# The product of v's summary with the input weight for all eight heads at once, over 64x32 pieces of the array and two PSUM banks

## The chip, the cores and the metric

One core of a Trainium2 chip runs the whole kernel. The metric is the device time of one execution in microseconds, taken from the first to the last instruction with what lies around them. Inputs and output lie in HBM; the two weights of each feed-forward layer come as 64-bit floats and are turned into 32-bit ones on the core.

## The reference, cut to what matters

For each of 8 batches and 8 heads, with 576 positions, head width 64 and 32 memory slots:

```
a   = softmax(phi)                      # 576 x 32
k_m = a.T @ k ;  v_m = a.T @ v          # 32 x 64 each: the summaries of k and v
attn = softmax(q @ k_m.T / 8)           # 576 x 32
x   = attn @ v_m                        # heads side by side: 576 x 512 per batch
h   = x @ w_in   (512 x 2048);  g = h * sigmoid(1.702 h);  y = g @ w_out   (2048 x 512)
out = the same kind of layer again, on y, with its own weights and sigmoid(h)
```

The kernel never forms x. It multiplies v's summary with the rows of w_in that belong to the head: for head i, v_m[i] (32 x 64) times rows 64i to 64i+63 of w_in. The eight results, 32 x 2048 each, stand over each other as a 256 x 2048 matrix W' of the batch, and h = attn (576 x 256) @ W'. This change is about how W' is computed.

## The kernel before, in words

The first layer runs in 256 numbered **slots**: 8 batches, two halves of 288 positions each, 16 blocks of 128 columns of w_in. In slot s, `first1` (line 386) issues 6 matmuls of 288 columns that give h of one block, `gate` lets ScalarE (lines 360, 364), VectorE (361) and GpSimd (366) make g in a high and a low part, and `second1` (line 398) issues the 12 matmuls of y for slot s-2. Everything else that a batch needs is planned into slots by tables of numbers: `at(slot, when, fn)` puts a call into slot `slot`, at one of the places "e" (ahead of the slot's h), "p" (behind the h, so on TensorE between h and y), "l" and "d" (loads, last). The attention of batch b+1 and its W' are worked out while batch b's slots run, so that a batch takes 32 slots. From slot 34 on the order of instructions is the written one on each engine; before that a scheduler moves them.

W' of a batch is 2048 columns wide and is made in pieces of 512: `c` = 0 to 3 is the piece of columns, `g` = 0, 1 the group of four heads. Before, there are eight products per batch, one for each (c, g). `wp_mm` (lines 273 to 277) takes one PSUM bank and issues two fp32 matmuls; each uses all 128 rows of the array and 64 of its columns. Their left side is the summary of two heads; since `kv_norm` (line 201) writes the summary twice, multiplied by a mask, the left side is block-diagonal and half of it is zero. `wp_hi` (ScalarE, line 281) and `wp_lo` (VectorE, line 285) then take the bank out as a high and a low part into `slab`.

The bank comes from `psa()` (line 90), a pool with **two** PSUM banks that are given out in turn and that all small matmuls of a batch share: the transposes of phi's maximum (`phi_max_t`, read by `phi_max_r`, line 149 on VectorE), its spreading (`phi_max_b`, line 157, read by `phi_sub`, line 164 on VectorE), `kv_mm` (line 185), `kv_t` (209), the transposes of q (`q_t`, line 220, read by `q_e` on ScalarE, line 224), `scores` (line 230, read by `soft1` on VectorE, line 242) and `wp_mm`. A bank comes free when its reader is done.

Per batch, counted from slot 32(b-1), where the slots of the batch ahead begin, the tables put the W' products at 20, 23, 27, 29, 31, 34, 38 and 39 (`WS`); transposes of q at 12, 16, 18, 20, 24, 27, 28 and 30; scores at 18, 23, 29 and 31; and, for the batch after the next, `phi_max_t` at 33, `phi_max_r` at 34, `phi_max_b` at 35, `phi_sub` at 36 and 37, `kv_mm` from 40 on. `soft2` (lines 255 to 260, VectorE) stands at 23, 26, 34 and 35. For batches 0 and 1 tables of their own (`W0`, `W1`) give the slots of the W' products.

w_in lies in SBUF as `w1` (128 x 4 x 2048, fp32). `w1_load` fetches a piece of 128 rows and 512 columns by one DMA, `w1_conv0` and `w1_conv1` (ScalarE, VectorE, GpSimd: lines 77, 78, 85, 86, 88) turn it into fp32. The loads stand in SyncE's queue among those of phi, k, v and q.

The few lines that say it:

```python
def psa():
    return ps_a.tile([128, 512], F32, tag="a", name="a")      # ps_a: bufs=2
WS = (20, 23, 27, 29, 31, 34, 38, 39)
SC = ((18, 19, 23), (23, 24, 26), (29, 30, 34), (31, 32, 35))
```

Of the kernel before, what the change touches and what calls it, by code (L numbers as in the profile page):

```python
# [10 lines left out]
I32 = mybir.dt.int32  # L11
# [3 lines left out]
ALU = mybir.AluOpType  # L15
# [6 lines left out]
def attn_moe_moe(ctx: ExitStack, tc: tile.TileContext, q, k, v, phi, w1i, w1o, w2i, w2o, out):  # L22
    nc = tc.nc
    B, H, S, D = q.shape
# [30 lines left out]
        return ap.bitcast(F32)  # L55


    def wload(src, rows, cols, t):

        if src.dtype == I64:  # L60
            nc.sync.dma_start(out=t.rearrange("p f w -> p (f w)"), in_=src[rows, cols].bitcast(I32))
            return t
        t = t.bitcast(F32).rearrange("p f w -> p (f w)")[:, 0:512]
        nc.sync.dma_start(out=t, in_=src[rows, cols])
        return t

    def raw():
        return moe.tile([128, 512, 2], I32, tag="raw", name="raw", bufs=2)
# [123 lines left out]
    def kv_norm(b, g):  # L192
        a = st.pop(("kvps", b, g))
        rs = att.tile([128, 2], F32, tag="rs", name="rs", bufs=2)
        nc.vector.tensor_scalar(out=rs[:, 0:1], in0=a[:, 2 * D:2 * D + 1], scalar1=1e-9, scalar2=None, op0=ALU.add)
        nc.vector.reciprocal(out=rs[:, 1:2], in_=rs[:, 0:1])
        kvb = att.tile([128, 2, 2, D], F32, tag="kvb", name="kvb")
        keep = mask.rearrange("p (s o) -> p s o", o=1).to_broadcast([128, 2, D])
        for i in range(2):
            x = a[:, i * D:(i + 1) * D].rearrange("p (o d) -> p o d", o=1).to_broadcast([128, 2, D])  # L200
            nc.vector.scalar_tensor_tensor(out=kvb[:, i], in0=x, scalar=rs[:, 1:2], in1=keep,
                                           op0=ALU.mult, op1=ALU.mult)
        st["kvb", b, g] = kvb

    def kv_t(b, g):
# [64 lines left out]
        t = attnT[b, hf]  # L270
        (nc.gpsimd if b else nc.vector).tensor_tensor(out=t[:, g, 1], in0=x, in1=rd(t[:, g, 0]), op=ALU.subtract)

    def wp_mm(b, c, g):
        a = st["wp", b, c, g] = psa()
        for i in range(2):
            nc.tensor.matmul(out=a[64 * i:64 * i + 64], lhsT=st["kvT", b, g][:, 1, 64 * i:64 * i + 64],
                             rhs=w1[:, 2 * g + i, c * 512:(c + 1) * 512], start=True, stop=True)

    def wp_hi(b, c, g):
        t = slab[b, c, g] = moe.tile([128, 2, 512], F32R, tag="slab", name="slab", bufs=8)  # L280
# [21 lines left out]

    def w1_load(n, kk, j):
        st["w1", kk, j] = wload(w1i, rows(kk), cols(j), early(n))

    def w1_conv0(kk, j):
        wconv0(st["w1", kk, j], w1[:, kk, cols(j)])
# [7 lines left out]
    def wo1_load(n, f):  # L315
        st["wo1", f] = wload(w1o, rows(f), cols(0), early(n))
# [384 lines left out]
    STGO = (1, 3, 4, 5)  # L701
    POOLF = (1, 3, 5, 7, 12, 14)

    W0 = (-4, -2, 1, 2, 10, 13, 14, 15)
    W1 = (18, 25, 28, 29, 32, 33, 39, 41)
    WS = (20, 23, 27, 29, 31, 34, 38, 39)

    Z1 = 5
    KV = ((8, 9, 10, 11, 12), (12, 13, 14, 15, 16))
# [14 lines left out]
    def plan_attention(b, z):  # L724
        for g in range(2):
            at(z - 2 + g, "e", phi_max, b, g)
        at(z + 1, "p", phi_max_t, b)
        at(z + 2, "e", phi_max_r, b)
        at(z + 3, "p", phi_max_b, b)
        for g in range(2):  # L730
            at(z + 4 + g, "e", phi_sub, b, g)
            at(z + 5 + g, "e", phi_exp, b, g)
            at(z + 6 + g, "e", phi_sum, b, g)
        for g, (k0, k1, n, t, e) in enumerate(KV):
            at(z + k0, "p", kv_mm, b, g, 0)
            at(z + k1, "p", kv_mm, b, g, 3)
            at(z + n, "e", kv_norm, b, g)
            todo.setdefault((z + t, "p"), []).insert(0, (kv_t, (b, g)))
            at(z + e, "e", kv_e, b, g)
        at(z + 10, "d", load_kv, b, 1, 0)  # L740
        at(z + 11, "d", load_kv, b, 1, 3)
        if b + 1 < B:
            at(z + 14, "d", load_kv, b + 1, 0, 0)
            at(z + 15, "d", load_kv, b + 1, 0, 3)
            at(z + 15, "d", load_phi, b + 1)
        for n in range(8):
            at(z + QS[n], "p", q_t, b, n // 4, n % 4)
            at(z + QS[n] + 1, "e", q_e, b, n // 4, n % 4)
            at(z + (QS[n - 2] if n > 1 else 2 + n), "d", load_q, b, n // 4, n % 4)
        for n, (p, s1, s2) in enumerate(SC):  # L750
            at(z + p, "p", scores, b, n // 2, n % 2)
            at(z + s1, "e", soft1, b, n // 2, n % 2)
            at(z + s1, "l", soft_exp, b, n // 2, n % 2)
            at(z + s2, "e", soft2, b, n // 2, n % 2)
            at(z + s2, "l", soft_hi, b, n // 2, n % 2)
            at(z + s2 + 1, "e", soft3, b, n // 2, n % 2)

    def plan_first(z):
# [9 lines left out]
        for g in range(2):  # L768
            at(z + 4 + g, "p", kv_mm, 0, g, 0)
            at(z + 4 + g, "p", kv_mm, 0, g, 3)  # L770
            at(z + 5 + g, "e", kv_norm, 0, g)
            at(z + 6 + g, "p", kv_t, 0, g)
            at(z + 7 + g, "e", kv_e, 0, g)
# [13 lines left out]
            at(s2, "l", soft_hi, 0, n // 2, n % 2)  # L787
            at(s2 + 1, "e", soft3, 0, n // 2, n % 2)

    def plan_wprime(b, n, s):  # L790
        a = (b,) + divmod(n, 2)
        at(s, "p", wp_mm, *a)
        at(s + 1, "e", wp_hi, *a)
        if b:
            at(s + 2, "e", wp_lo, *a)
        else:
            at(s + 1, "l", wp_lo, *a)

    make_identity(nc, ident)
    nc.vector.memset(ones, 1.0)  # L800
# [26 lines left out]
    for b in range(B):  # L827
        if b:
            plan_attention(b, 32 * (b - 1) + (Z1 if b == 1 else 0))
        for n in range(8):  # L830
            plan_wprime(b, n, (W0, W1)[b][n] if b < 2 else 32 * (b - 1) + WS[n])
    for n, p in enumerate(seq):
        o = CONV[n]
        w = len(p) == 2
# [174 lines left out]
```

## Time and profile before

| | us |
|---|---|
| median of 3 runs | 1595.64 (1595.29 to 1596.5) |
| profiled execution | 1593.76 |
| its span, first to last instruction | 1592.0 |
| slots of the first layer, h of slot 0 to the last h | 34.9 to 816 |
| busy TensorE / VectorE / ScalarE / GpSimd in the span | 1514.9 / 1007.5 / 765.0 / 556.0 |

An execution has a stretch of loading and converting up to about 110 us, then the slots of the first layer at TensorE's pace up to about 820 us, then the second layer. In the rows below L386 is h, L398 is y, L276 is the W' product. A row "x4" of L276 is one product: each fp32 matmul shows as two passes. Times are from the start of the span.

### The profile page before, as it was taken

To read this page: it belongs to the slowest core of one execution; us is meant where nothing else is said; L and a number is where in the kernel's file an instruction comes from. 1 tells how busy PE (TensorE), PEld (TensorE's weight loads), DVE (VectorE), ACT (ScalarE), POOL (GpSimd) and SP (SyncE) were. 2 spreads that over 40 slices of the span, in tenths; PEclk is the share of its full clock that TensorE was granted. 3 is DMA by queue.
4 is the path that set the end of the run, shared out by engine and by line. 5 is a ranking of instruction groups with operands and counts; after the bars stand their busy time and mean duration, and the time that the engine had idled before them with its cause. 6 is when DMAs were issued, how large, how long until landed. Compare 5 with 4: busy or idle time off the path is not lost. (4 is left out here: it accounts for less than half of the span.)

```text
span 1592.0 us, 29090 instructions
## 1 busy us (share of the span) xinstructions
PE 1514.9 (95%) x11104; PEld 1405.9 (88%) x11104; DVE 1007.5 (63%) x1560; ACT 765.0 (48%) x1539; POOL 556.0 (35%) x461
## 2 busy tenths in 40 slices
PE   4799999999999999999999999999977999999998
PEld 2578898988989898898999999999977999999998
DVE  6995546365463645634567655665677678677675
ACT  4674444454554544544555554554654434344342
POOL 2764334344443444433322311311126234044040
PEclk9799999999999999999999999999998999999999
DMA  9652252524425253312125424424454514515330
GB/s 281 184 163 60 56 132 86 142 71 116 119 87 155 75 139 93 93 39 88 42 66 167 140 105 152 142 105 151 154 181 137 188 50 151 163 60 176 108 102 31
DMA packets 174156, 189.08 MB, mean 119 GB/s; under 512 B 50112, under 2 KB 161728, under 8 KB 174016
## 3 DMA queue, kind: packets, MB, share of 16 engines
q1 hardware_dynamic: 174016, 187.22, 38.5%
q8 instruction: 87, 1.43, 0.4%
q14 instruction: 53, 0.43, 0.1%
HBM read 122.16 MB, written 65.01 MB: 118 GB/s over the span
## 5 line engine op out<-in xcount | busy, mean ns | idle before, releaser
L398 PE MATMUL y<-gh,wo 128*128 128x288 f32 x2048 | 460.0, 301 | 0.3 <-ACT gh L364 0.3
L642 PE MATMUL p<-wq,op 128*128 128x256 f32 x3024 | 373.5, 285 | 20.9 <-ACT op L629 10.5
L642 PEld LDWEIGHTS p<-wq,op 128*128 128x128 f32 x3024 | 366.1, 191 | 28.3 <-DVE op L438 15.8
L398 PEld LDWEIGHTS y<-gh,wo 128*128 128x128 f32 x2048 | 341.3, 188 | 52.1 <-issue 25.8
L366 POOL TENSOR_TENSOR gl<-g,gh 128x288 fp32r<-128x288 f32 x256 | 225.4, 881 | 424.6 <-ACT gh L364 377.2
L398 PE MATMUL y<-gl,wo 128*128 128x288 f32 x1024 | 301.8, 295 | 2.7 <-POOL gl L366 2.7
L361 DVE SCALAR_TENSOR_TENSOR g<-g,h 128x288 f32<-128x288 f32 x256 | 114.7, 449 | 288.1 <-ACT g L360 286.7
L438 DVE TENSOR_TENSOR op<-r,op 128x768 fp32r<-128x768 f32 x168 | 217.5, 1323 | 102.3 <-ACT op L629 97.1
L386 PE MATMUL h<-attnT,slab 128*128 128x288 f32 x1536 | 249.7, 297 | 13.7 <-ACT attnT L266 5.7
L386 PEld LDWEIGHTS h<-attnT,slab 128*128 128x128 f32 x1536 | 218.5, 189 | 18.8 <-ACT attnT L266 6.8
L533 PE MATMUL xb<-xq,wq 128*128 128x384 f32 x1152 | 219.5, 339 | 11.4 <-ACT e L566 6.3
L629 ACT CAST op<-r 128x768 fp32r<-128x768 f32 x168 | 138.0, 835 | 187.1 <-DVE r L438 86.3
L533 PEld LDWEIGHTS xb<-xq,wq 128*128 128x128 f32 x1152 | 200.4, 188 | 18.9 <-ACT e L583 9.7
L398 PEld LDWEIGHTS y<-gl,wo 128*128 128x128 f32 x1024 | 192.7, 188 | 4.6 <-POOL gl L366 3.6
L360 ACT ACTIVATE g<-h 128x288 f32<-128x288 f32 x256 | 104.2, 407 | 189.6 <-PE h L386 182.7
L364 ACT CAST gh<-g 128x288 fp32r<-128x288 f32 x256 | 110.7, 433 | 167.6 <-DVE g L361 167.5
L533 PE MATMUL y<-xq,wq 128*128 128x384 f32 x864 | 166.4, 337 | 2.5 <-ACT e L594 2.5
L533 PEld LDWEIGHTS y<-xq,wq 128*128 128x128 f32 x864 | 151.8, 188 | 2.8 <-ACT e L594 2.8
L542 ACT ACTIVATE gq<-e 128x384 f32<-128x384 f32 x144 | 75.0, 525 | 131.9 <-DVE e L435 131.9
L435 POOL TENSOR_TENSOR r<-r 128x768 f32<-128x768 f32 x24 | 57.2, 2411 | 212.5 <-DMA r<-gs 212.4
L547 DVE SCALAR_TENSOR_TENSOR gq<-gq,e 128x384 f32<-128x384 f32 x144 | 99.9, 698 | 32.7 <-ACT gq L542 27.5
L438 POOL TENSOR_TENSOR xq<-xr,xq 128x768 fp32r<-128x768 f32 x20 | 38.5, 1924 | 153.9 <-ACT xq L523 153.9
(111 smaller groups left out, 1523.6 us busy)
## 6 DMA issues: line engine op xcount, KB each, us to landing
gs<-gq SPq DMA_DIRECT2D x192, 192.0 KB, 1.9
r<-gs SPq DMA_DIRECT2D x192, 192.0 KB, 3.9
raw<-in_moe_w_out_dram SPq DMA_DIRECT2D x24, 512.0 KB, 4.0
raw<-in_moe_w_in_dram SPq DMA_DIRECT2D x18, 512.0 KB, 4.7
xr<-xs SPq DMA_DIRECT2D x24, 384.0 KB, 5.0
out_dram<-o SPq DMA_DIRECT2D x24, 384.0 KB, 3.2
q<-in_q_dram SPq DMA_DIRECT2D x124, 72.0 KB, 2.5
kv<-in_k_dram SPq DMA_DIRECT2D x30, 288.0 KB, 4.4
```

The source lines that it names most:

```text
L360: nc.scalar.activation(out=t[:, :n], in_=h[:, :n], func=ACTF.Tanh, scale=c)
L361: nc.vector.scalar_tensor_tensor(out=t[:, :n], in0=t[:, :n], scalar=1.0, in1=h[:, :n], op0=ALU.add, op1=ALU.mult)
L364: nc.scalar.copy(out=gh[:, :n], in_=t[:, :n])
L366: nc.gpsimd.tensor_tensor(out=gl[:, :n], in0=t[:, :n], in1=rd(gh[:, :n]), op=ALU.subtract)
L386: nc.tensor.matmul(out=h[:, :HS], lhsT=slab[b, f // 4, g][:, wi, f0:f0 + 128], rhs=x[:, g, xi], start=(g == 0 and n == 0), stop=(g == 1 an ...
L398: nc.tensor.matmul(out=ybank[d][:, :HS], lhsT=w[:, wi, d * 128:(d + 1) * 128], rhs=gg[gi][:, :HS], start=(f == fa and n == 0), stop=(f == ...
L438: eng.tensor_tensor(out=out, in0=a, in1=b, op=ALU.subtract)
L533: nc.tensor.matmul(out=out, lhsT=w[:, s, wi, f0:f0 + 128], rhs=x[:, s, xi], start=(start and s == 0 and k == 0), stop=(s == 1 and k == 2), ...
L542: nc.scalar.activation(out=t, in_=h, func=ACTF.Tanh)
L547: nc.vector.scalar_tensor_tensor(out=t, in0=t, scalar=1.0, in1=h, op0=ALU.add, op1=ALU.mult)
L629: nc.scalar.copy(out=t[:, :, 0], in_=s)
L642: nc.tensor.matmul(out=out[:, d], lhsT=t[:, u, gi, d * 128:(d + 1) * 128], rhs=w[:, u, wi], start=(start and d != 1 and p == 0 and u == 0 ...
```

## The change

`wp_mm` does both groups of heads in one call: two banks at once, and eight fp32 matmuls per piece of 512 columns, one per head. Each uses 64 rows and 32 columns of the array: head 4g+j lies on rows 64g to 64g+63 and writes partitions 32j to 32j+31 of bank g. There are four products per batch in place of eight. For that, `w1` is laid out anew (`w1[64g : 64g+64, j]` holds the rows of head 4g+j), so that a load of w_in is two DMAs of 64 partitions, and the summary of v is written twice without the mask. The tables are new: per batch the four products stand in slots 21, 25, 34 and 37. `wp_lo` follows `wp_hi` in the same slot.

```diff
+    def wload(src, rows, cols, t, at=slice(0, 128)):
+            nc.sync.dma_start(out=t[at].rearrange("p f w -> p (f w)"), in_=src[rows, cols].bitcast(I32))
 ...
-        for i in range(2):
-            x = a[:, i * D:(i + 1) * D].rearrange("p (o d) -> p o d", o=1).to_broadcast([128, 2, D])
-            nc.vector.scalar_tensor_tensor(out=kvb[:, i], in0=x, scalar=rs[:, 1:2], in1=keep,
-                                           op0=ALU.mult, op1=ALU.mult)
+        x, y = (a[:, i * D:(i + 1) * D].rearrange("p (o d) -> p o d", o=1).to_broadcast([128, 2, D]) for i in range(2))
+        nc.vector.scalar_tensor_tensor(out=kvb[:, 0], in0=x, scalar=rs[:, 1:2], in1=keep, op0=ALU.mult, op1=ALU.mult)
+        nc.vector.tensor_scalar(out=kvb[:, 1], in0=y, scalar1=rs[:, 1:2], scalar2=None, op0=ALU.mult)
 ...
-    def wp_mm(b, c, g):
-        a = st["wp", b, c, g] = psa()
-        for i in range(2):
-            nc.tensor.matmul(out=a[64 * i:64 * i + 64], lhsT=st["kvT", b, g][:, 1, 64 * i:64 * i + 64],
-                             rhs=w1[:, 2 * g + i, c * 512:(c + 1) * 512], start=True, stop=True)
+    def wp_mm(b, c):
+        for g in range(2):
+            st["wp", b, c, g] = psa()
+        for j in range(4):
+            for g in range(2):
+                r = slice(64 * g, 64 * g + 64)
+                nc.tensor.matmul(out=st["wp", b, c, g][32 * j:32 * j + 32], lhsT=st["kvT", b, g][r, 1, 32 * j:32 * j + 32],
+                                 rhs=w1[r, j, c * 512:(c + 1) * 512], start=True, stop=True)
 ...
+        t = early(n)
+        for g in range(2):
+            r = slice(256 * g + 64 * kk, 256 * g + 64 * kk + 64)
+            st["w1", kk, j] = wload(w1i, r, cols(j), t, slice(64 * g, 64 * g + 64))
 ...
-    W0 = (-4, -2, 1, 2, 10, 13, 14, 15)
-    W1 = (18, 25, 28, 29, 32, 33, 39, 41)
-    WS = (20, 23, 27, 29, 31, 34, 38, 39)
+    W0 = (-2, 2, 13, 15)
+    W1 = (26, 30, 37, 39)
+    WS = (21, 25, 34, 37)
 ...
+        at(s, "p", wp_mm, b, c)
+        for g in range(2):
+            at(s + 1, "e", wp_hi, b, c, g)
+            at(s + 1, "e" if b else "l", wp_lo, b, c, g)
```

What moves on the engines is shown at three places. The first is TensorE around slot 130, which is slot 34 of the third batch in the steady part (b = 4). Before, with the product's two matmuls (L276) between h (L386) and y (L398), and `phi_max_b` (L157) in the next slot:

```order
L386 MATMUL h<-attnT,slab 128x288 x5
L276 MATMUL a<-w_83,kvT 64x512 [waits DVE_49]
L276 MATMUL a<-w_83,kvT 64x512
L398 MATMUL y_5559<-gh,wo_306 128x288 [waits DVE_49,Activation_49]
...
L386 MATMUL h<-attnT,slab 128x288 x6
L157 MATMUL a<-ident,nm 96x128 [waits DVE_49,PE_49]
```

And now (h is L394, y is L406, the product L280):

```order
L394 MATMUL h<-attnT,slab 128x288 x5
L280 MATMUL a<-w_83,kvT 32x512 [waits PE_49]
L280 MATMUL a<-w_83,kvT 32x512 [waits DVE_49,PE_49]
L280 MATMUL a<-w_83,kvT 32x512 x6
L406 MATMUL y_5648<-gh,wo_312 128x288 [waits Activation_49]
...
L394 MATMUL h<-attnT,slab 128x288 x6
L157 MATMUL a<-ident,nm 96x128 [waits DVE_49]
```

The second matmul of the product now waits for VectorE: the first one writes the bank of g = 0, the second the bank of g = 1, which `phi_max_t` of slot 33 had.

The second place is VectorE in the same slots: `phi_max_r` (L149), the gate (L361 before, L369 now), `soft2` (L255 to L260), `wp_lo` (L285 before, L289 now) and `phi_sub` (L164). Before:

```order
L149 TENSOR_REDUCE nm<-a 128x2
L361 SCALAR_TENSOR_TENSOR g<-g,h 128x288 [waits Activation_49]
L255 TENSOR_REDUCE sm<-nat 128x9
...
L260 STREAM_TRANSPOSE at<-nat 128x288 [waits DVE_49,Pool_49]
L361 SCALAR_TENSOR_TENSOR g<-g,h 128x288 [waits Activation_49]
L285 TENSOR_TENSOR slab<-a,slab 128x512 [waits PE_49]
L164 TENSOR_TENSOR phi<-phi,a 96x768 [waits PE_49]
```

And now:

```order
L149 TENSOR_REDUCE nm<-a 128x2
L369 SCALAR_TENSOR_TENSOR g<-g,h 128x288 [waits Activation_49]
L255 TENSOR_REDUCE sm<-nat 128x9
...
L260 STREAM_TRANSPOSE at<-nat 128x288 [waits DVE_49,Pool_49]
L289 TENSOR_TENSOR slab<-a,slab 128x512 [waits Activation_49] x2
L369 SCALAR_TENSOR_TENSOR g<-g,h 128x288 [waits Activation_49]
L164 TENSOR_TENSOR phi<-phi,a 96x768 [waits PE_49]
```

Both `wp_lo` of the piece now stand one after the other behind `soft2` and ahead of the gate.

The third place is SyncE's queue at the start, with the first loads of w_in (L61). Before:

```order
L109 DMA kv<-in_v_dram 96x4x192
L61 DMA rawe<-in_moe_w_in_dram 128x1024 x2
L119 DMA kve<-in_k_dram 96x2x192
```

And now:

```order
L109 DMA kv<-in_v_dram 96x4x192
L61 DMA rawe<-in_moe_w_in_dram 64x1024 x4
L119 DMA kve<-in_k_dram 96x2x192
```

Each load of w_in is two DMAs of half the rows; there are 16 such loads in all.

## Rows read from the trace of the kernel before

**Rows 1.** The profile page, part 1: busy time (share of the span) and instructions of each engine.

```profile
PE 1514.9 (95%) x11104; PEld 1405.9 (88%) x11104; DVE 1007.5 (63%) x1560; ACT 765.0 (48%) x1539; POOL 556.0 (35%) x461
```

**Rows 2.** Busy time of each engine by stretch (start:end, length, then PE, PEld, DVE, ACT, POOL with instruction counts, granted clock, DMA share, GB/s).

```profile
0.00:50.00 50.00, 22.31 (x151) 13.48 (x151) 37.36 (x67) 24.45 (x45) 17.83 (x19) 0.82 0.86 248
50.00:110.00 60.00, 51.62 (x354) 40.17 (x354) 59.39 (x94) 42.60 (x90) 42.84 (x35) 0.95 0.63 183
...
324.00:420.00 96.00, 96.00 (x762) 85.67 (x761) 51.94 (x105) 46.58 (x110) 39.39 (x43) 1.00 0.39 106
420.00:516.00 96.00, 96.00 (x763) 85.67 (x762) 51.58 (x104) 45.39 (x108) 40.42 (x44) 1.00 0.39 108
```

**Rows 3.** TensorE in order of time in slots 112 to 120, its h, q, scores and W' rows alone (start, duration, line, x count); the start of an h row is the start of a slot.

```profile
402.24 0.95 PE L386 MATMUL h<-attnT,slab 128*128 128x288 f32 x6
403.03 0.41 PE L220 MATMUL a<-ident,q 96*128 96x96 f32 x3
404.88 0.95 PE L386 MATMUL h<-attnT,slab 128*128 128x288 f32 x6
407.25 0.95 PE L386 MATMUL h<-attnT,slab 128*128 128x288 f32 x6
...
410.70 0.96 PE L386 MATMUL h<-attnT,slab 128*128 128x288 f32 x6
413.09 0.99 PE L386 MATMUL h<-attnT,slab 128*128 128x288 f32 x6
413.92 0.41 PE L220 MATMUL a<-ident,q 96*128 96x96 f32 x3
414.26 1.08 PE L276 MATMUL a<-w,kvT 128*64 128x512 f32 x4
...
416.94 0.96 PE L386 MATMUL h<-attnT,slab 128*128 128x288 f32 x6
...
421.73 0.95 PE L386 MATMUL h<-attnT,slab 128*128 128x288 f32 x6
422.61 0.71 PE L230 MATMUL a<-qT,kvT 128*64 128x288 f32 x4
423.15 1.03 PE L276 MATMUL a<-w,kvT 128*64 128x512 f32 x4
425.79 0.43 PE L386 MATMUL h<-attnT,slab 128*128 128x288 f32 x2
```

**Rows 4.** TensorE in order of time at three places: one matmul of a product alone (two passes, early in the program), a whole product (four passes) in slot 130, and `kv_mm`, whose matmuls use 96 rows and four groups of 32 columns.

```profile
85.31 1.07 PE L276 MATMUL a<-w,kvT 128*64 128x512 f32 x2
86.32 1.06 PE L386 MATMUL h<-attnT,slab 128*128 128x288 f32 x6
...
455.46 0.96 PE L386 MATMUL h<-attnT,slab 128*128 128x288 f32 x6
456.35 1.08 PE L276 MATMUL a<-w,kvT 128*64 128x512 f32 x4
457.36 0.40 PE L398 MATMUL y<-gh,wo 128*128 128x288 f32 x1
...
459.04 0.95 PE L386 MATMUL h<-attnT,slab 128*128 128x288 f32 x6
459.82 0.60 PE L157 MATMUL a<-ident,nm 128*96 128x128 f32 x4
...
382.36 0.86 PE L185 MATMUL a<-kv,phi 96*32 96x128 f32 x24
383.15 0.38 PE L189 MATMUL a<-ones,es 96*128 96x2 f32 x2
```

**Rows 5.** VectorE in order of time in slots 130 and 131 (start, duration, line; in brackets what ended idle time before it).

```profile
454.76 0.96 DVE L377 TENSOR_SCALAR o<-y 128x288 f32<-128x288 f32 x2
455.64 0.44 DVE L255 TENSOR_REDUCE sm<-nat 128x9 f32<-128x288 f32 x1
...
457.47 0.32 DVE L149 TENSOR_REDUCE nm<-a 128x2 f32<-128x192 f32 x1
...
460.51 0.48 DVE L260 STREAM_TRANSPOSE at<-nat 128x288 f32<-128x288 f32 x1 [0.69 <-POOL attnT L271]
460.91 0.42 DVE L361 SCALAR_TENSOR_TENSOR g<-g,h 128x288 f32<-128x288 f32 x1
461.25 0.68 DVE L285 TENSOR_TENSOR slab<-a,slab 128x512 fp32r<-128x512 f32 x1
```

**Rows 6.** Slot 133, which is slot 37 of the batch: the start of its h on TensorE, and the second `phi_sub` on VectorE with the weight conversion ahead of it.

```profile
464.22 0.96 PE L386 MATMUL h<-attnT,slab 128*128 128x288 f32 x6
...
465.91 0.69 DVE L86 SCALAR_TENSOR_TENSOR stg<-raw,stg 128x512 int32<-128x512 int32 x1
466.52 0.94 DVE L164 TENSOR_TENSOR phi<-phi,a 96x768 f32<-96x768 f32 x1
```

**Rows 7.** `phi_max_r` on VectorE in slot 98, slot 34 of the batch before, where a weight conversion lies ahead of it; and TensorE's rows of that slot.

```profile
363.66 0.32 DVE L149 TENSOR_REDUCE nm<-a 128x2 f32<-128x192 f32 x1
...
359.79 0.96 PE L386 MATMUL h<-attnT,slab 128*128 128x288 f32 x6
360.67 1.08 PE L276 MATMUL a<-w,kvT 128*64 128x512 f32 x4
```

**Rows 8.** Slot 40, the end of batch 1's W': TensorE's `kv_mm`, and VectorE's end of `soft2` with the `wp_lo` behind it.

```profile
186.28 0.86 PE L185 MATMUL a<-kv,phi 96*32 96x128 f32 x24
...
187.71 0.48 DVE L260 STREAM_TRANSPOSE at<-nat 128x288 f32<-128x288 f32 x1 [0.69 <-POOL attnT L271]
188.11 0.42 DVE L361 SCALAR_TENSOR_TENSOR g<-g,h 128x288 f32<-128x288 f32 x1
188.45 0.68 DVE L285 TENSOR_TENSOR slab<-a,slab 128x512 fp32r<-128x512 f32 x1
```

**Rows 9.** ScalarE behind the transposes of q in slot 116: the copy that frees the bank.

```profile
415.44 0.39 ACT L224 COPY qT<-a 128x288 f32<-128x288 f32 x1
415.73 0.59 ACT L281 CAST slab<-a 128x512 fp32r<-128x512 f32 x1
```

**Rows 10.** SyncE's queue at the start: issues of the first loads (start, time in the queue, x count).

```profile
3.62 1.50 SPq L61 DMA_DIRECT2D rawe<-in_moe_w_in_dram  x2
...
14.38 0.90 SPq L61 DMA_DIRECT2D rawe<-in_moe_w_in_dram  x2
```

More of the change, by code (lines that the diff above doesn't have):

```diff
@@ L55, in rd @@
         return ap.bitcast(F32)
-    def wload(src, rows, cols, t):
+    def wload(src, rows, cols, t, at=slice(0, 128)):
         if src.dtype == I64:
-            nc.sync.dma_start(out=t.rearrange("p f w -> p (f w)"), in_=src[rows, cols].bitcast(I32))
+            nc.sync.dma_start(out=t[at].rearrange("p f w -> p (f w)"), in_=src[rows, cols].bitcast(I32))
             return t
         t = t.bitcast(F32).rearrange("p f w -> p (f w)")[:, 0:512]
-        nc.sync.dma_start(out=t, in_=src[rows, cols])
+        nc.sync.dma_start(out=t[at], in_=src[rows, cols])
         return t
@@ L303, in w1_load @@
     def w1_load(n, kk, j):
-        st["w1", kk, j] = wload(w1i, rows(kk), cols(j), early(n))
+        t = early(n)
+        for g in range(2):
+            r = slice(256 * g + 64 * kk, 256 * g + 64 * kk + 64)
+            st["w1", kk, j] = wload(w1i, r, cols(j), t, slice(64 * g, 64 * g + 64))
     def w1_conv0(kk, j):
@@ L788, in plan_first, with plan_wprime @@
             at(s2 + 1, "e", soft3, 0, n // 2, n % 2)
[L790 to L797, printed above, removed]
+    def plan_wprime(b, c, s):
+        at(s, "p", wp_mm, b, c)
+        for g in range(2):
+            at(s + 1, "e", wp_hi, b, c, g)
+            at(s + 1, "e" if b else "l", wp_lo, b, c, g)
     make_identity(nc, ident)
@@ L829, in attn_moe_moe @@
             plan_attention(b, 32 * (b - 1) + (Z1 if b == 1 else 0))
-        for n in range(8):
+        for n in range(4):
             plan_wprime(b, n, (W0, W1)[b][n] if b < 2 else 32 * (b - 1) + WS[n])
```

## Prediction

> **What bounds the kernel now.** I began with the page's busy times: TensorE is busy 95% of the span, VectorE 63%, ScalarE 48% [rows 1]. An average over stages says little, so next came busy time by stretch [rows 2]. In the steady part, 324 to 516 us, TensorE is busy 96.00 of 96 us twice over and VectorE a little over half. There every microsecond taken off TensorE's queue comes off the time, unless TensorE then waits for something. From 50 to 110 us it is the other way: VectorE is busy 59.39 of 60 us, TensorE 51.62, so less work for TensorE buys nothing there. The third view is TensorE in order of time [rows 3], which gives the price of each kind of slot, and the fourth VectorE's rows at the places where the change makes TensorE wait [rows 5 to 8].
>
> **What is removed.** Differences between starts of h [rows 3]: a plain slot is 407.25 - 404.88 = 2.37 us; with a transpose of q 404.88 - 402.24 = 2.64; with that and scores 410.70 - 407.25 = 3.45, so scores cost 0.81. A slot with a transpose and a product is 416.94 - 413.09 = 3.85, so a product costs 3.85 - 2.64 = 1.21. Behind scores it is cheaper: 425.79 - 421.73 = 4.06, less 2.37 and 0.81, is 0.88. Of a batch's eight products three stand behind scores (slots 23, 29, 31), five don't: 3 x 0.88 + 5 x 1.21 = 8.7 us per batch.
>
> **What is added.** Four products per batch, none in a slot with scores or a transpose. What one costs hangs on whether eight matmuls run side by side in the array. For groups of columns the rows show it: one matmul alone, two passes, holds TensorE from 85.31 to 86.32, 1.01 us; a whole product, four passes on two groups of columns, holds it from 456.35 to 457.36, also 1.01 us [rows 4]. Each pass is then some 0.50 us, and the second group is free. `kv_mm` uses four groups of columns: 24 passes of 128 columns take 383.15 - 382.36 = 0.79 us, 0.132 per round of four, where a quarter of 0.50 is 0.126. So four groups cost what one does. No row shows two groups of **rows**: `kv_mm` has 96 rows in one piece. The bounds: if both halves run together, a new product costs 1.21 + 0.04 (six more starts, an estimate, several times what `kv_mm` shows) = 1.25; if the halves follow each other, two more passes, 1.25 + 2 x 0.50 = 2.25. I take 1.25, as all that the rows show of separate pieces is that they run together. Then a batch pays 5.0 in place of 8.7: **3.7 us less per batch**, for batches 1 to 7 25.9 us.
> The Trainium skill ("TensorE: Matmul & The Clock Gate", Part 3) gives four row tiles 3.07 times the speed of one and all sixteen pieces 10.6 times; by it the halves overlap, and the sum would stand as it is with 1.25. No run here shows that yet.
>
> **What it makes wait.** The product now takes both banks of the pool at once, so it waits for the later of two readers, and what follows waits for it. Slot by slot of a batch:
>
> *Slot 21* follows a transpose of q in slot 20, whose bank ScalarE's copy frees. In slot 116 the copy ends at 415.44 + 0.39 = 415.83, 2.74 after the slot's start of 413.09 [rows 3, 9]. The product of slot 21 would want the bank 2.64 + 0.89 = 3.53 after that start (0.89 is 456.35 - 455.46, rows 4). No wait. *Slot 25* is the same behind slot 24: none.
>
> *Slot 34* is the dear one. The bank of g = 1 was that of `phi_max_t` in slot 33, and its reader L149 stands on VectorE behind two copies of y and a whole `soft2`. It ends at 457.47 + 0.32 = 457.79, while the product starts at 456.35 [rows 4, 5]. The copies of y wait for slot 33's last matmuls, so this lateness is tied to the slot and stays: the second matmul waits **1.44 us**. Nothing else on TensorE can pass it. In slot 98 a weight conversion makes L149 later still: 363.66 + 0.32 - 360.67 = 3.31 [rows 7]. Batches 2 to 6 have a batch behind them whose maximum is taken, so 4 x 1.44 + 3.31 = 9.1 us.
>
> *Slot 35*: `phi_max_b` (L157) wants the bank of g = 0, which the first `wp_lo` frees. Before, it came at 459.82; with 1.48 more it comes at 461.3. VectorE is at `soft2` until 460.51 + 0.48 = 460.99, and 0.68 for the `wp_lo` makes 461.67 [rows 4, 5]. 0.4 per batch, 2.0 in all.
>
> *Slot 37*: the bank of g = 1 is the one that `phi_sub` reads. In slot 133 its second half ends at 466.52 + 0.94 = 467.46 behind a conversion; the product would want it at 464.22 + 0.89 + 1.9 of the waits ahead = 467.0 [rows 6]. 0.5 there, nothing where no conversion lies.
>
> *Batch 1, slot 40*: the last product stands in slot 39, and `kv_mm` of slot 40 wants its first bank. VectorE's `wp_lo` stands behind a `soft2` that ends at 187.71 + 0.48, so the bank is free at 188.19 + 0.68 = 188.87, and `kv_mm` started at 186.28 [rows 8]: 2.6 us, once. The 1.25 that TensorE comes later through slot 39 and the two more `wp_lo` (2 x 0.68) ahead on VectorE cancel.
>
> Conversions fall into slots 21, 25 and 35 of some batch too; I put 2 us for all of these, by slot 133's 0.5. Together 9.1 + 2.0 + 0.5 + 2.6 + 2 = **16.2 us given back**.
> The Trainium skill ("TensorEngine Tiling (Array Packing)", Restrictions and Gotchas) warns that row tiling raises PSUM pressure, as row tiles must write different banks. The rows above are that rule at work in a pool of two.
>
> **The start.** Batch 0's products lie where VectorE is full, so their saving is taken as 0; it could be 3.7 at best. Against it, w_in's 16 loads become 32 issues on SyncE at 1.50 / 2 = 0.75 us or 0.90 / 2 = 0.45 [rows 10], ahead of k, v and q; for the four loads that all else waits for that is up to 3 us, and the first product now needs four loads where it needed two. The bytes are the same, and VectorE has 50 - 37.36 = 12.6 us idle ahead of 50 us [rows 2]. I take 0, between -4 and +4. The second copy of the summary without its mask is one VectorE instruction for one: 0. ScalarE and VectorE take out the same number of banks.
>
> **The sum.** -25.9 + 16.2 = -9.7. The profiled execution of 1593.76 would be 1584.1. It ran 1.9 under the median of 1595.64, and against that I say **1586**. The second layer is untouched and starts earlier by what the first one saves.
>
> **The rivals.**
> *The halves follow each other* (slower). Nothing in the rows excludes it. Four passes in a row make a product 2.25: 28 x 1.0 = 28 more, 1614. If only one pass of four falls out of step, 28 x 0.5 = 14, 1600. It decides the sign from 9.7 / 28 = 0.35 us more per product on: one single pass of 0.50 out of step is enough.
> *The bank waits are mostly not there*. For it: VectorE has fewer products to serve between slots 26 and 33 and could be ahead at slot 34; against it: L149's lateness hangs on slot 33's own y. Then 25.9 less some 4 leaves -22, and with a little from the start 1572.
> *The start eats it*. The scheduler orders the first 34 slots anew; if VectorE's full stretch begins some 8 to 10 us later (a late load, a first product that waits), the result is no change, 1595. That is against the idle 12.6 us, but the stretch to 50 us has DMA at 0.86 [rows 2].
>
> **How the numbers follow.** The forecast 0.58, within 1579 to 1593. The halves in a row 0.20, 0.14 of it at 1614 and 0.06 at 1600. Few bank waits 0.12. The start 0.10. The range leaves out 1614 and the outer ends: 1568 to 1604. A measurement of this kernel can tell 0.2%, 3.2 us, from no change: faster is under 1592.4, slower over 1598.8. Faster 0.56 + 0.12 = 0.68; the same 0.02 + 0.08 = 0.10; slower 0.20 + 0.02 = 0.22.
>
> **What would show it.** In the changed profile: plain slots still 2.37; a slot with a product and no wait 3.62; a product from its second matmul to y in 1.0 to 1.1 us. Slot 34 of batches 2 to 6 near 5.1, with L149 as the releaser of the product; a gap ahead of `kv_mm` in slot 40. It is wrong if products of slots 21 and 25 hold TensorE 1.5 or 2 us (rows in turn), if slot 34 is 3.6 (no bank wait), or if slot 34's h stands at another time already in batch 1 (the start).

## The result

The change is slower: **1611.35 us** (median of 4 runs, 1611.03 to 1616.73) against 1595.47 for the kernel before on the same chip; the ratio is 1.0107, 95% interval 1.0085 to 1.0129. The forecast was 1586, faster, with a range to 1604. The profiled execution took 1611.23, its span is 1609.4.

In the changed kernel h is L394 and y L406, the product L280, its copies L285 and L289; other lines named here are those of before where no new one is given. First the page's busy times, against [rows 1].

```profile
PE 1509.1 (94%) x11360; PEld 1405.7 (87%) x11360; DVE 1009.1 (63%) x1560; ACT 764.6 (48%) x1539; POOL 552.3 (34%) x461
```

TensorE is busy for 5.8 us less and the span is 17.4 longer, so it stands idle for 23.2 us more: waits ate more than the smaller work gave. Busy time by stretch, against [rows 2], says where.

```profile
0.00:50.00 50.00, 18.84 (x135) 10.50 (x135) 35.51 (x64) 22.74 (x42) 15.65 (x17) 1.00 1.00 246
50.00:110.00 60.00, 50.74 (x366) 39.59 (x367) 51.52 (x83) 35.69 (x78) 36.13 (x32) 1.00 0.63 150
324.00:420.00 96.00, 93.60 (x781) 83.82 (x779) 51.73 (x102) 45.15 (x108) 39.04 (x42) 0.98 0.38 107
420.00:516.00 96.00, 94.70 (x796) 84.88 (x795) 51.85 (x105) 46.03 (x110) 40.07 (x43) 1.00 0.40 109
```

The granted clock of 1.00 in the first two rows is no reading for the time ahead of 66.58 us, where the clock's records of this run begin: at 64.55 us the last 14 passes of a product still take 1.95 us, where all 16 take 1.09 in the steady part.

Two things are new. From 50 to 110 us VectorE, which was the full engine there, is busy 51.52 in place of 59.39: it now waits. And TensorE is no longer full in the steady part.

TensorE in slots 117 to 119, against [rows 3]: a slot with a product and no wait, then a plain one.

```profile
432.47 0.96 PE L394 MATMUL h<-attnT,slab 128*128 128x288 f32 x6
433.36 1.09 PE L280 MATMUL a<-w,kvT 64*32 64x512 f32 x16
...
436.06 0.95 PE L394 MATMUL h<-attnT,slab 128*128 128x288 f32 x6
438.44 0.95 PE L394 MATMUL h<-attnT,slab 128*128 128x288 f32 x6
```

436.06 - 432.47 = 3.59, less the plain slot's 2.38, is 1.21 us for all eight heads. That is what a product of two pairs of heads cost before. The eight pieces run side by side, rows and columns.

The bank waits stand where they were forecast. Slot 130, against [rows 4]; slot 98, against [rows 7]; and slot 40, against [rows 8]:

```profile
469.65 0.96 PE L394 MATMUL h<-attnT,slab 128*128 128x288 f32 x6
470.54 1.04 PE L280 MATMUL a<-w,kvT 64*32 64x512 f32 x2
472.34 1.09 PE L280 MATMUL a<-w,kvT 64*32 64x512 f32 x14 [0.76 <-DVE nm L149]
...
475.04 0.95 PE L394 MATMUL h<-attnT,slab 128*128 128x288 f32 x6
...
372.64 0.96 PE L394 MATMUL h<-attnT,slab 128*128 128x288 f32 x6
373.53 1.04 PE L280 MATMUL a<-w,kvT 64*32 64x512 f32 x2
376.97 1.81 PE L280 MATMUL a<-w,kvT 64*32 64x512 f32 x14 [2.40 <-DVE nm L149]
...
381.25 0.95 PE L394 MATMUL h<-attnT,slab 128*128 128x288 f32 x6
...
196.17 0.95 PE L394 MATMUL h<-attnT,slab 128*128 128x288 f32 x6
199.95 1.51 PE L185 MATMUL a<-kv,phi 96*32 96x128 f32 x24 [2.83 <-DVE slab L289]
201.39 0.61 PE L406 MATMUL y<-gh,wo 128*128 128x288 f32 x1
...
204.44 1.64 PE L394 MATMUL h<-attnT,slab 128*128 128x288 f32 x6
```

Slot 130 takes 5.39. Slot 98 takes 8.61 and slot 40 8.27, more than their waits explain: after each the same matmuls take longer (14 passes of the product 1.81 instead of 1.09, `kv_mm` 1.51 instead of 0.86). The reason is in the granted clock (the number behind the instruction counts) of the stretches behind those two waits, and of one ahead:

```profile
180.00:196.00 16.00, 16.00 (x133) 13.07 (x132) 11.42 (x19) 7.20 (x16) 3.24 (x4) 1.00 0.04 10
199.70:206.50 6.80, 6.55 (x54) 5.79 (x58) 1.16 (x3) 1.09 (x3) 1.55 (x2) 0.50 0.34 87
...
377.20:380.60 3.40, 3.40 (x22) 1.89 (x9) 2.61 (x7) 1.84 (x4) 1.77 (x2) 0.50 0.69 178
```

TensorE had been busy throughout at 2.4 GHz (16.00 of 16 us ahead of slot 40), stood for 2.83 and 2.40 us, and then ran at 1.2 GHz for 6.83 and 3.41 us by the clock's records. These show two more such stretches: 3.41 us behind a wait of 2.05 us in slot 159, and 6.83 us at the start, from 124.61, behind waits of 0.70 and 1.78 us. The kernel before has none between 57 and 1196 us.

What TensorE waited for from slot 24 to 800 us (line, releaser, us in total, times, longest), the five largest, where the kernel before has 0.5 us in all from its slot 24 on:

```profile
PE a L280 <- DVE nm L149: 4.8, 5, 2.4
PE a L185 <- DVE slab L289: 2.8, 1, 2.8
PE a L230 <- ACT qT L224: 2.1, 1, 2.1
PE a L157 <- DVE slab L289: 1.7, 1, 1.7
PE y L406 <- DVE o L385: 0.9, 1, 0.9
...
```

The time by turns of 32 slots (one batch each), from starts of h; the numbers in the last column are durations of slots:

| slots | before | after | difference | what lies in it |
|---|---|---|---|---|
| start of slot 32 | 159.7 | 171.2 | +11.4 | the start |
| 32 to 64 | 99.0 | 102.2 | +3.2 | slot 40 8.27, with the slow stretch; slot 53 4.92 |
| 64 to 96 | 96.1 | 94.4 | -1.7 | slot 66 5.18 |
| 96 to 128 | 95.7 | 97.0 | +1.3 | slot 98 8.61, with the slow stretch |
| 128 to 160 | 96.3 | 100.7 | +4.4 | 130 5.39; 133 5.12; 149 4.46; 159 7.48, clock 0.5 in it too |
| 160 to 192 | 95.6 | 96.9 | +1.3 | 162 5.18; 163 4.80; 178 4.39; 185 4.12 |
| 192 to 224 | 95.7 | 93.8 | -1.9 | slot 194 5.18 |
| 224 to 254 | 75.2 | 74.2 | -1.0 | no wait |

The two turns in which little but the forecast waits fell, 64 to 96 and 192 to 224, gained 1.7 and 1.9, what the forecast's own terms give (3.7 - 1.44 - 0.4 = 1.9). So two things have to be explained: 11 us at the start, and some 13 us of waits and slow stretches in the other turns, beyond those that were forecast.

### The profile page after: what moved, and what is told of

Read it like the earlier page. It is cut to its first block, busy times and chain, and to the rows that moved or that the text cites. A ratio compares the mean times of both kernels' runs of the same rounds, so it can differ in the third digit from the quotient of the medians.

```text
span 1609.4 us, 29639 instructions
## 1 busy us (share of the span) xinstructions
PE 1509.1 (94%) x11360; PEld 1405.7 (87%) x11360; DVE 1009.1 (63%) x1560; ACT 764.6 (48%) x1539; POOL 552.3 (34%) x461
## 5 line engine op out<-in xcount | busy, mean ns | idle before, releaser
L406 PE MATMUL y<-gh,wo 128*128 128x288 f32 x2048 | 465.1, 303 | 1.9 <-ACT gh L372 1.0
L406 PEld LDWEIGHTS y<-gh,wo 128*128 128x128 f32 x2048 | 345.1, 190 | 44.4 <-issue 22.6
L374 POOL TENSOR_TENSOR gl<-g,gh 128x288 fp32r<-128x288 f32 x256 | 221.0, 864 | 440.6 <-ACT gh L372 412.1
L406 PE MATMUL y<-gl,wo 128*128 128x288 f32 x1024 | 303.8, 297 | 5.3 <-POOL gl L374 5.3
L369 DVE SCALAR_TENSOR_TENSOR g<-g,h 128x288 f32<-128x288 f32 x256 | 114.9, 449 | 286.8 <-ACT g L368 286.6
L394 PE MATMUL h<-attnT,slab 128*128 128x288 f32 x1536 | 250.9, 299 | 5.9 <-DVE slab L289 2.6
L541 PE MATMUL xb<-xq,wq 128*128 128x384 f32 x1152 | 219.8, 339 | 12.3 <-ACT e L574 6.3
L394 PEld LDWEIGHTS h<-attnT,slab 128*128 128x128 f32 x1536 | 220.4, 191 | 10.9 <-DVE g L369 3.2
L406 PEld LDWEIGHTS y<-gl,wo 128*128 128x128 f32 x1024 | 195.0, 190 | 6.1 <-POOL gl L374 6.0
```

What stands on the lines that cost most here:

```text
L369: nc.vector.scalar_tensor_tensor(out=t[:, :n], in0=t[:, :n], scalar=1.0, in1=h[:, :n], op0=ALU.add, op1=ALU.mult)
L374: nc.gpsimd.tensor_tensor(out=gl[:, :n], in0=t[:, :n], in1=rd(gh[:, :n]), op=ALU.subtract)
L394: nc.tensor.matmul(out=h[:, :HS], lhsT=slab[b, f // 4, g][:, wi, f0:f0 + 128], rhs=x[:, g, xi], start=(g == 0 and n == 0), stop=(g == 1 an ...
L406: nc.tensor.matmul(out=ybank[d][:, :HS], lhsT=w[:, wi, d * 128:(d + 1) * 128], rhs=gg[gi][:, :HS], start=(f == fa and n == 0), stop=(f == ...
L541: nc.tensor.matmul(out=out, lhsT=w[:, s, wi, f0:f0 + 128], rhs=x[:, s, xi], start=(start and s == 0 and k == 0), stop=(s == 1 and k == 2), ...
```

## The experiments

The first loads on SyncE's queue (start, time in the queue, count), against [rows 10]:

```profile
3.41 3.08 SPq L61 DMA_DIRECT2D rawe<-in_moe_w_in_dram  x4
16.05 2.39 SPq L61 DMA_DIRECT2D rawe<-in_moe_w_in_dram  x4
27.92 7.31 SPq L61 DMA_DIRECT2D rawe<-in_moe_w_in_dram  x8
```

Four theories followed from the trace. **A**: loads into 64 partitions move bytes slower, so all is late. **B**: the start is late because a product needs two banks and four loads at once (before, a product of one group of heads needs one bank and two loads). **C**: in the steady part, bank waits and the slower clock behind the longest of them ate the gain. **D**: VectorE is full in slots 28 to 40, so waits only change places. "Late at slot 24" below is the start of its h against the kernel before.

**1. One load in place of two, the layout of the change.**

```
- t[64g:64g+64] <- w_in[256g+64kk : +64]          # two loads
+ t <- w_in.rearrange("(g k r) x -> k g r x")[kk]  # one load, 128 partitions
```

> The changed kernel with each load of w_in as one DMA that writes all 128 partitions (two blocks of 64 rows of the source), all else as changed. Theory A (the start is late because a DMA into 64 partitions moves its bytes more slowly): slot 24 starts near 137 to 140 us in place of 148.4, and the time is 1600 to 1603. Theory B (the start is late because the new tables want two banks and all four loads at the first product): slot 24 stays near 148 and the time at 1611.

Measured 1718.74 (1.0768, 1.0750 to 1.0786). Its DMA engines in 40 slices of 0 to 60 us (share in tenths, then GB/s), and what was loaded there:

```profile
DMA  0499998111131414417141411111133131224357
GB/s 0 44 286 218 227 232 188 51 52 52 52 118 64 135 49 132 130 55 216 53 129 44 128 45 63 55 49 55 52 92 97 50 98 49 77 85 118 76 86 259
...
rawe<-in_moe_w_in_dram SPq DMA_DIRECT2D x6, 512.0 KB
```

Where only such a load is under way, a tenth of the engines' time is used, about two of sixteen, and 49 to 55 GB/s flow. The Trainium skill ("DMA: Bandwidth & Descriptors", Why a DMA increments its semaphore by 16 and not by 1) says that a transfer gets the largest number of engines, up to 16, that divides the slowest dimension of both its patterns; here the source's is g = 2, and the trace agrees. So this run put a larger fault in the place of the one that it was to take away (slot 24 is 119 us late) and does not test A; its expectation is a miss.

**2. The old layout, loads and shape (two heads each, 64 columns), but both groups in one call by the change's tables.**

```
- for j in range(4): for g in range(2): matmul(64 rows, 32 columns)
+ for g in range(2): for i in range(2): matmul(128 rows, 64 columns)   # before's w1, loads, mask
```

> The kernel before (its layout, its loads, its mask, its two matmuls per group on 128 rows and 64 columns) with the changed kernel's tables: both groups of heads in one call, two banks at once. Tables alone. Theory A: slot 24 near 136 to 138, a product costs 1.21 + 1.01 = 2.2 us, the bank waits of slots 34, 35, 37 and 40 are there as in the changed kernel, time 1605 to 1612. Theory B: slot 24 near 148, time 1615 to 1622.

1615.65 (1.0124, 1.0109 to 1.0139); late at slot 24: 4.9 us, 140.9 where A had 136 to 138 and B 148. Loads as before take most of the lateness away; a part stays with the tables. The time is above A's 1605 to 1612: this shape saves TensorE nothing, and the bank waits are there all the same (the first layer ends 19.9 us late).

**3. The change's layout, loads and shape, one group per product by the old tables.**

```
- def wp_mm(b, c): two banks, for j, for g          W0, W1, WS of the change
+ def wp_mm(b, c, g): one bank, for j (64 x 32)     W0, W1, WS of before
```

> The changed kernel's layout, loads and summary without mask, but one group of heads per product (four matmuls on 64 rows and 32 columns, one bank) at the tables of before. Loads alone, with a product that should cost 1.21 as before. Theory A: slot 24 at 142 to 148, time 1601 to 1607. Theory B: slot 24 near 136, time 1595 to 1597.

1613.21 (1.0112, 1.0097 to 1.0127). Late at slot 24 by 13.8, 14.6 at slot 64, 18.6 at the end of the layer. With neither two banks nor new tables the start is as late as in the change, so the two banks aren't needed for it. The time is 6 us above A's 1601 to 1607, a miss. And the run doesn't show A alone: it keeps the layout, in which a product needs four loads, the other half of B.

**4. Steady products at other slots.**

```
- WS = (21, 25, 34, 37)
+ WS = (21, 25, 32, 38)
```

> The changed kernel with two of a batch's four products moved, from slots 34 and 37 to 32 and 38, where both banks are free by the plan. Theory C (the waits for a bank, and the clock that falls behind the long ones, ate the gain of batches 2 to 6): slots 66, 98, 130, 162 and 194 lose their 1.6 to 5 us, slot 133 its 1.5, slot 163 its 2, no granted clock of 0.5 at 377 us; time 1596 to 1600. Theory D (VectorE is the bound between slots 28 and 40 once products are cheap): the same waits appear in other slots, time 1606 to 1611.

1603.35 (1.0044, 1.0030 to 1.0058), 8 us less than the change. The waits in the batch's slots 34 and 37 and the slow stretch at 377 are gone, and the layer's end comes 9.8 us earlier. C holds for these. It is short of 1596 to 1600 because some 7 us of new waits came: 0.6 to 1.1 us each in slots 68, 69, 99, 129, 134, 160 and 165, and more in 149, 178 and 185 (slot 134 takes 4.72 in place of 3.58). So D is right for a part.

**5. The kernel before, only its loads of w_in split.**

```
+ t = early(n)
+ for g in range(2):
+     wload(w_in[128kk+64g : +64], t[64g : 64g+64])   # same rows, same places
```

> The kernel before, with each load of a piece of w_in issued as two loads of the same rows into 64 partitions each, and nothing else. Theory A (loads into 64 partitions move bytes slower, and the start waits for them): slot 24 begins 12 to 14 us later than in the kernel before, as in the run with one group per product (+13.8), and most of it stays: 1605 to 1612 us. Theory B (the start is late because a product needs two banks and all four pieces of its columns): slot 24 within 2 us of before, 1594 to 1598 us.

1606.52 (1.0067, 1.0052 to 1.0082): 10.7 us for nothing but the split. Slot 24 is 9.0 late and every slot after it 8.8 to 9.1: a pure delay. The miss is only in its size (9 against 12 to 14 at slot 24). B alone is out as the cause of the whole. The 4.8 us between this run and run 3 go with the layout; that they are B's four loads is likely, and not shown.

The last link of the delay stands in slot 22, TensorE first and then GpSimd:

```profile
138.55 0.40 PE L401 MATMUL y<-gl,wo 128*128 128x288 f32 x1 [3.26 <-POOL gl L369]
...
134.80 1.71 POOL L338 TENSOR_TENSOR wo<-stg,wo 128x512 fp32r<-128x512 f32 x1
136.47 1.27 POOL L88 TENSOR_TENSOR stg<-stg,rawe 128x512 int32<-128x512 int32 x1
137.71 2.08 POOL L369 TENSOR_TENSOR gl<-g,gh 128x288 fp32r<-128x288 f32 x2
```

GpSimd's part of the gate (`gl`) stands behind conversions of w_out that have come late too, and TensorE's y waits for it; behind the wait the clock is at 1.2 GHz for 3.41 us. The kernel before is through with its last such conversion at 124.4 us and has no such wait. The change has it at 143.36, 2.89 us.

**6. Even and odd heads on the row halves.** A piece of w_in is then 128 rows in a row again and one load, with the shape and tables of the change.

```
- r = slice(64*g, 64*g+64);  rhs = w1[r, j]           # two loads per piece
+ e = 64*((j+g) % 2);        rhs = w1[e:e+64, 2*g + j//2]   # one load per piece
+ kv_mm: group 1 writes head j to rows 32*(j^1); mask and sums accordingly
```

> The changed kernel with the heads divided over the array's row halves by even and odd head instead of first four and last four, so that a piece of w_in is again 128 rows in a row and one load into 128 partitions; in the second group the rows of k, v and the scores stand with each pair of heads exchanged, for which the sums of that group take four matmuls instead of one. The product keeps its eight 64x32 pieces and two banks, the tables are the changed kernel's. Theory A: slot 24 no more than 5 us after that of before (as with the old shape and loads under the same tables, +4.9) instead of +12.3, and 1599 to 1607 us, 1604 the likeliest (1611.4 less 7.4). Theory B: the late start stays, 1609 to 1613 us.

1606.48 (1.0069, 1.0054 to 1.0084), 4.9 us under the change and inside A's range; late at slot 24: 6.2, a little over A's 5. Against run 2 the only large difference is the shape: 9.2 us less.

**7. The change, products of batches 1 to 7 moved.**

```
- W1 = (26, 30, 37, 39);  WS = (21, 25, 34, 37)
+ W1 = (24, 27, 30, 38);  WS = (21, 25, 32, 38)
```

> The changed kernel with the products of batches 2 to 7 at slots 21, 25, 32, 38 of their turn (as in the run that moved them, 1603.4 us) and those of batch 1 at 24, 27, 30, 38 instead of 26, 30, 37, 39. Theory C (waits for a bank or a slab, and the lower clock that follows the longest of them): the wait of 2.83 us at slot 40 and the stretch at granted clock 0.5 behind it (6.83 us) both go, and the time falls by the wait and half of the stretch, 2.8 + 3.4: 1597 us, 1596 to 1600. If the clock falls without the wait, or costs nothing: 1600 to 1601. Theory D (VectorE bound there, so that the wait comes back at another slot): 1602 to 1605.

1596.85 (1.0007, 0.9997 to 1.0016). Slot 40 in this run:

```profile
195.33 0.96 PE L394 MATMUL h<-attnT,slab 128*128 128x288 f32 x6
196.22 0.86 PE L185 MATMUL a<-kv,phi 96*32 96x128 f32 x24
...
198.70 0.95 PE L394 MATMUL h<-attnT,slab 128*128 128x288 f32 x6
```

Without the wait the clock stays. Slots 40 and 41 take 6.95 us; in run 4, with a wait of 2.82 and 3.41 us at the lower clock behind it, they took 11.38. The difference of 4.4 is the wait and half of the slow stretch (1.7), as C had it. Another 1.2 in the same turn is batch 1's product that went from slot 37 to slot 30, ahead of slot 32.

**8. Runs 6 and 7 together.**

> Both edits together: even and odd heads on the row halves with one load for each piece of w_in, and the products moved for batches 1 to 7. If A and C hold side by side, 1597 less 7.4: 1590 us, 1586 to 1594, under the kernel before (1595.5). If the late start and the waits were one and the same delay, only the larger of the two comes back: 1596 to 1602.

1593.55 (0.9987, 0.9978 to 0.9997), inside the expected range, but 3.3 us under run 7, where 7.4 had been expected. In the two profiled executions the first layer ends 7.8 us earlier (810.3 against 818.1), so there the loads' part is whole; why the medians keep less is open. (What lies behind the first layer takes 775 to 780 us in the profiled executions, 784.5 in run 10's, so a few us between two runs need not come from the first layer.) Late at slot 24: 5.7. TensorE's waits from 95 to 125 us there are led by one of `kv_mm` for the banks that the product of slot 13 still holds:

```profile
PE a L186 <- DVE slab L293: 6.6, 1, 6.6
...
```

**9. Run 8, the third product of batch 0 earlier.**

```
- W0 = (-2, 2, 13, 15)
+ W0 = (-2, 2, 11, 15)
```

> The last kernel (even and odd heads on the row halves, one load for each piece of w_in, products of batches 1 to 7 moved) with the third product of batch 0 at slot 11 instead of 13, so that its two banks are free before the first kv_mm of batch 1 (slot 13). Theory B (the rest of the late start, +5.7 us at slot 24, is a wait for the product's second bank): the wait of 6.56 us before kv_mm at 100 to 107 us and the stretch at granted clock 0.5 from 102.5 go, slot 24 begins at 135 to 138 us, and the time is 1588 us, 1585 to 1591. Rival (VectorE, busy 9.5 of 10 us there, sets the start): the delay comes back behind slot 16, slot 24 stays at 140 to 142 us, 1591.5 to 1595 us.

1594.47 (0.9991, 0.9978 to 1.0004), late at slot 24: 5.8. The wait moved, to the next product, which now waits for the sums' normalisation:

```profile
PE a L284 <- DVE kvb L205: 5.5, 1, 5.5
...
```

Slot 24 and the time are where the rival had them (VectorE sets the start): moving this wait brought nothing. That VectorE does set it is not shown by that.

**10. Run 9, the second layer's conversions one slot later.** In run 9 ScalarE and TensorE stood thus in slot 53 (ScalarE's rows, then TensorE's; L373 and L369 are the gate, L227 is `q_e`):

```profile
227.49 0.66 ACT L77 ACTIVATE stg<-raw 128x512 f32<-128x512 f32 x1 [2.69 <-DMA raw<-in_moe_w_in_dram]
228.05 0.65 ACT L78 ACTIVATE raw<-raw 128x512 int32<-128x512 uint32 x1
228.60 0.38 ACT L369 ACTIVATE g<-h 128x288 f32<-128x288 f32 x1
229.51 0.43 ACT L373 CAST gh<-g 128x288 fp32r<-128x288 f32 x1 [0.52 <-DVE g L370]
229.85 0.39 ACT L227 COPY qT<-a 128x288 f32<-128x288 f32 x1
...
227.99 1.04 PE L284 MATMUL a<-w,kvT 64*32 64x512 f32 x2
230.29 1.09 PE L284 MATMUL a<-w,kvT 64*32 64x512 f32 x14 [1.26 <-ACT qT L227]
```

The conversion at the head of ScalarE's queue waits 2.69 us for its load; the copy that frees the second bank stands behind it.

```
- at(s + 2, "e", w2_conv0, m, n); at(s + 2, "l", w2_conv1, m, n)
+ at(s + 3, "e", w2_conv0, m, n); at(s + 3, "l", w2_conv1, m, n)
```

> The same, with each conversion of a piece of the second layer's weights (ScalarE, VectorE, GpSimd; every fifth slot) one slot later behind its load, which still stands two slots ahead of the store. In the last kernels' traces ScalarE stands with the conversion at its head, waiting for the load, while the gate and the copy q_e behind it hold up the product's second bank (slots 53, 149) and the scores (159). Theory C: these waits (2.6 + 1.5 us, and at 159 2.3 us with a stretch at clock 0.5 behind it) go for the most part: 3 to 6 us less than the kernel before it in this list. Rival: the conversions meet other slots' products instead, and the time is within 2 us of that kernel or above it.

1582.67 (0.9928, 0.9911 to 0.9946), 11.8 under run 9, twice what was expected. In the profiled executions the first layer ends 8.2 us earlier, though slot 24 is 8.2 us late here, 2.4 more than in run 9. The same slot now:

```profile
229.22 0.39 ACT L227 COPY qT<-a 128x288 f32<-128x288 f32 x1
230.61 0.69 ACT L77 ACTIVATE stg<-raw 128x512 f32<-128x512 f32 x1 [1.00 <-DMA raw<-in_moe_w_in_dram]
...
230.44 1.09 PE L284 MATMUL a<-w,kvT 64*32 64x512 f32 x16
```

The 16 passes run in one piece, and turn 128 to 160 takes 92.7 us where run 9 took 99.8. The waits of slots 53, 85, 159 and 185 are gone; slot 149 still takes 4.57 (5.07 in run 9), and slot 95 has a new wait (4.72). Whether the same edit would help the kernel before was not tried.

**11. The kernel before, each load split by columns.**

```
+ for i in range(2): dma(t[:, 256i : 256i+256], w_in[rows, cols half i])   # 128 partitions each
```

> The kernel before, with each load of a piece of w_in as two loads of half its columns into all 128 partitions, in place of the two loads into 64 partitions that cost 10.7 us alone. If it is the 64 partitions that cost: 1594 to 1598 us, slot 24 within 2 us of before. If it is the number of loads (twice as many issues and waits on the queue): 1603 to 1608 us, slot 24 about 9 us late. Something between if the half-long packets (2048 bytes) move slower too.

1595.42 (1.0000, 0.9990 to 1.0009); slot 24 0.3 late. Twice as many loads cost nothing; it is the 64 partitions. From 10 to 20 us (DMA share and GB/s last), first the kernel before, then run 5, then this run:

```profile
10.00:20.00 10.00, 8.06 (x104) 6.09 (x104) 7.99 (x12) 4.83 (x8) 1.99 (x2) 1.00 1.06 318
```

```profile
10.00:20.00 10.00, 6.97 (x84) 4.75 (x83) 8.28 (x12) 4.43 (x7) 1.73 (x2) 1.00 1.07 236
```

```profile
10.00:20.00 10.00, 8.08 (x104) 6.00 (x103) 7.98 (x12) 4.46 (x8) 2.19 (x2) 1.00 1.09 305
```

In all three the DMA engines are busy throughout (share 1.06 to 1.09); in run 5 they move a quarter less meanwhile. It is the single packet that takes longer: those of 4096 bytes that start in this stretch take 165 ns (median) in the kernel before and 281 in run 5, those of 2048 bytes in this run 89. The Trainium skill ("SBUF — State Buffer", Can I just issue two DMAs to hit both halves?) says that only one transfer over all 128 partitions reaches all 16 ports, and that two at once, one at each half, moved only 6% more than one. The trace agrees in direction, with 236 GB/s against 318; its ratio is not tested here, as other loads run beside w_in's.

**12. Run 10, both late products of batch 0 ahead of `kv_mm`.**

```
- W0 = (-2, 2, 11, 15)
+ W0 = (-2, 2, 10, 12)
```

> The fastest kernel so far (conversions one slot later, 1582.7 us) with the last two products of batch 0 at slots 10 and 12 instead of 11 and 15, both ahead of the first kv_mm of batch 1, whose sums hold one of the two banks from slot 13 to their normalisation in slot 15. With the product at 13, kv_mm waited 6.6 us for it (slot 24 at 141.8 us); with it at 11, the next one at 15 waited 5.5 us for the normalisation of those sums (slot 24 at 141.9). Theory B (the rest of the late start is the second bank, wanted while kv_mm holds one): neither wait is left, slot 24 begins at 135 to 139 us, and the time is 1577 to 1581 us. Rival (VectorE's conversions set the start whatever the products' slots are): slot 24 stays at 141 to 145 us and the time at 1581 to 1585 us.

1582.46 (0.9921, 0.9907 to 0.9935), no faster than run 10 (1582.67); late at slot 24: 7.4, against 8.2 there. The 6.6 and 5.5 us waits are gone and the lateness is not: B misses, and the numbers are again where the rival had them. This run and run 10 beat both kernels.

## Why the prediction was wrong, by its steps

**The start (the step that failed).** "I take 0, between -4 and +4", because "the bytes are the same". The bytes were, the rate wasn't: with the split loads alone (run 5) 236 GB/s flow at 10 to 20 us where 318 flow with whole ones, and the start of the change came 11.4 us late at slot 32. Run 5 shows 9.0 of it with nothing but the split; run 11 shows that the number of issues, which I had priced, costs nothing. The prediction's own last sign came too: h of slot 34 stands at 176.7 in place of 167.5. VectorE's 12.6 us idle ahead of 50 us were no cover: it did 35.51 us of work there against 37.36, and 51.52 against 59.39 in the next 60, so at 110 us it is 9.7 us of work behind. The rival "the start eats it" had that (VectorE 8 to 10 us later, a late load named in passing), at 0.10. Part of the 11.4 is the clock: the 6.83 us at 1.2 GHz from 124.61 cost up to half of that.

Of the rest, both groups in one call under the new tables make slot 24 4.9 late without split loads (run 2), 5.7 to 8.2 in runs 6, 8, 9, 10 and 12. With the split it is 12.3 and not 4.9 + 9.0, and with the split and the new layout but without the tables 13.8 (run 3): the parts overlap. Which part of the tables it is stays open; two moves of batch 0's products did not bring it back.

**The product: right.** 1.21 against 1.25; in turn 64 to 96 the 1.7 gained and the waits of slots 66 and 67 (1.60 and 0.3) make 3.6, where 3.7 per batch was forecast. The rival with 1614 us had nearly the right number by luck: its halves that follow each other are not there.

**Bank waits: places right, prices short.** Against slots without a wait (3.58), slot 34 of the batch cost 1.60 three times, 1.81, and 5.03 in slot 98: 11.6 against 9.1. The wait in 98 was 3.3 as forecast; 1.7 is half of the 3.41 us at the lower clock. Slot 35: 2.8 against 2.0, of which 2.0 in slot 163. Slot 37: 1.5 against 0.5. Slots 40 and 41: 12.8 where 7.0 were due without a wait, 5.8 against 2.6; the wait itself was 2.83, the rest the lower clock. "Conversions", 2 us: 7.7, of which 3.6 in slot 159 (7.48 against 3.22 without a wait, less the 0.7 that the kernel before loses there) and the others in 53, 85, 149, 178 and 185. Run 10 shows what most of these are: a conversion waits for its load at the head of ScalarE's queue, and what frees the bank stands behind it; in run 10 all of them but 149's are gone. That is 13.2 us more than the 16.2. Of the -25.9, batch 1's half, 1.9, fell ahead of slot 32, where it buys nothing. -9.7 + 13.2 + 1.9 = +5.4, and +5.5 was measured from slot 32 to 254.

So two things were left out. The loads' rate alone turns the sign: -9.7 + 11.4 = +1.7. And the three waits of 2.83, 2.40 and 2.05 us were paid again by the clock behind them, 3.4 + 1.7 + 1.7 = 6.8 of the 13.2; most of the rest is conversions, which had been priced by one slot.

## What to carry over

Price a load by the partitions it reaches, not by its bytes alone: if a new layout needs half-height loads, look for another assignment of rows (here even and odd heads) that leaves them whole. Where an instruction comes to need two buffers of a pool of two, list the readers of both, and what stands at the head of their engines' queues. Price a new wait on a full TensorE by its length and by what the granted clock may do behind it (here half of 3.41 or 6.83 us).

## What the runs showed of the hardware

- Eight fp32 matmuls on pieces of 64 rows and 32 columns, in two banks, take 1.21 us of TensorE, what four passes over two pieces of 128 rows and 64 columns take.
- From 10 to 20 us, with all loads together, 318 GB/s flow where w_in comes by loads into 128 partitions, 305 where each is two loads by columns, and 236 where each is two loads into 64 partitions, the engines as busy. One load whose source has an outer dimension of 2 gets 49 to 55 by itself.
- TensorE, busy for many us at 2.4 GHz, fell to 1.2 GHz after standing 2.83, 2.40 and 2.05 us (slots 40, 98, 159) and stayed there for 3.41 or 6.83 us, which cost half of that. After 2.89 us without work up to 143.36, in the start, no fall is recorded; in run 4 the same gap, 2.88 us, has 3.41 us at 1.2 GHz behind it, and in run 7, 2.86 us, has none. The length of the gap alone doesn't tell.
